# Inverse transform's second stage in two-step pieces, residual sum and stores moved behind it, and a new set of due times

## The chip, the cores and the metric

The kernel runs on one core of one Trainium2 chip. The metric is the device time of one execution in microseconds (us), compared as medians over runs. The core's engines are named as in the profile: PE is the matrix engine (PEld its weight loads), DVE the vector engine, ACT the scalar engine with its function tables, SP the queue that issues all DMA transfers here. POOL does nothing of weight.

## The reference, cut to what matters

The input is one sequence `x` of 2048 positions by 512 channels. Its layer norm feeds two branches: a state-space convolution, whose kernel of 2048 taps per channel is summed from 128 complex exponentials and applied by FFT, and a token-and-channel mixer with two small MLPs. Their product is added to the input.

```python
xn = _layernorm(x, axis=-1)
s = _A_ref(xn, ...)     # K = einsum(C, exp(dt A l), dt B).real; y = irfft(rfft(K) * rfft(u)); y + u * Dskip
g = _silu(_B_ref(xn, B_w1, B_w2, B_w3, B_w4))   # spatial-shift mixing, then the channel MLP
return x + s * g
```

## The kernel before

Position is split as (t, r, s): s has 16 values and is called a step here, r has 4, t has 32. A tile over 128 partitions holds r and t; `X` (line 459) holds all 16 steps by 512 channels in SBUF and is rewritten in place: input, then its layer norm, then the mixer's residual stream, then its Silu, then the result.

The program is not issued in the order in which it is written. Every call on an engine is recorded in a `Plan` with an estimated cost, the tiles it touches and a due time (`due(t)`, line 536). `Plan.order` (line 220) then runs a list scheduler: on the engine that comes free first it picks, among the operations whose inputs its model holds ready, the one with the smallest due time, and adds penalties: `SWITCH` for an ACT operation that needs another function table, `PREFER` or `AVOID` for an operation that either ACT or DVE may do (class `Either`). `LAND` and `PAD` are the model's latencies of a DMA and of a signal between engines. The order that comes out is fixed; at run time each engine works through its own list and waits on signals. So a changed due time or buffer moves rows on all four engines.

The stages, in words:

- Loads, layer norm, `h_pair`, `u_stage1`, `hs_pair`: token mixing, and the first stage of the input's transform (written to DRAM as `scr_Ud`).
- `tables(hf)` for two halves of the channels (256 each), eight chunks of 32 channels per half: ACT and DVE make tables of exponentials, sines and cosines (tiles `mag`, `pt`, `kt`, `eg`), PE multiplies them into the convolution kernel (`pc<-kt`, `pc<-pt`), which goes to DRAM (`scr_Kda`, `scr_Kdb`).
- `kstage1(hf)`: first transform stage of that kernel, through DRAM (`ksl` in, `scr_Kfa`/`scr_Kfb` out).
- `products(hf)`: second stage of both transforms, complex product, first inverse stage; its results go to DRAM (`scr_Zda`, `scr_Zdb`). The second half has eight units.
- `mlp(g)`, g = 0..7: the channel MLP on two steps of `X` each (`pb<-x1T,w3h`, `ghl`, `pa<-w4h,ghl`, then `X<-pa`). It fills PE between the stages above.
- `gate(g)`: Silu of two steps. `finish(hf, q)`: second inverse stage, product with the gate, residual sum, store.

`finish` works on four steps of one half of the channels. It loads 2 x 512 KB of `scr_Zda` or `scr_Zdb` into `zin` (a ring of two buffers of 1 MB, `zinr`), and four slices of the input into `xr` (a ring of two, `xrr`); PE fills a pair of PSUM banks; DVE multiplies both into `X`, adds `xr`, and four stores of 128 KB follow, in runs of 1 KB. The pairs alternate between the banks `pc` and `pd` (`pp_pair`, line 524). A read of a DRAM scratch tensor waits for all writes to that tensor, so no `scr_Zdb` load starts before the last unit of `products(1)` has stored.

Of the kernel before, what the change touches and what calls it, by code (L numbers as in the profile page):

```python
# [10 lines left out]
F32 = mybir.dt.float32  # L11
# [8 lines left out]
P = 128  # L20
L = 2048
D = 512
# [72 lines left out]
SAME = {"PE": 0.0, "ACT": 0.13, "DVE": 0.1, "SP": 0.0}  # L95
TABLE_LOAD = 1.41
DMA_RATE = 300e3
LAND, PAD = 4.17, 0.21
BASE, FINE, END = 16512, 19840, 229368

KGC = 3.25
SWITCH = 70.05
PREFER, AVOID = 182.71, 8.67
PV, T0, TC = 91.3, -48.6, 81.82
M0, MC, WC = 233.6, 235.8, 0.05
H0, HC, SC = -706.8, 114.13, 0.09
KA, PA, PAC, FA = 159.4, -391.4, 0.1, 834.5
KB, PB, PBC, FB = 90.8, 491.3, 0.06, 203.3
FC = 0.06


def mlp_due(g, jp):
# [3 lines left out]
class Plan:  # L116
# [103 lines left out]
    def order(self):  # L220
# [17 lines left out]
        while len(out) < len(ops):  # L238
# [4 lines left out]
            for o in pools[e]:  # L243
                if o.ready <= t + 0.02:
                    v = o.vt
                    if e == "ACT" and o.table and o.table != table:
                        v += SWITCH
                    if len(o.alts) > 1:
# [140 lines left out]
def kernel(  # L389
# [8 lines left out]
    plan = Plan(nc)  # L398
    V, A, T, Q = [Engine(plan, e) for e in ("DVE", "ACT", "PE", "SP")]
    E = Either(plan)  # L400

    xv = u[0].rearrange("(t r s) d -> r t s d", r=4, s=S)
    ov = out[0].rearrange("(t r s) d -> r t s d", r=4, s=S)
# [5 lines left out]
    DH = D // 2  # L409
    Kd = [dram.tile([P, NCH, L2, 4], F32, name=f"scr_Kd{h}") for h in "ab"]  # L410
    K1d = [dram.tile([4, 2 * NG, L2, DH // 4], F32, name=f"scr_Kf{h}") for h in "ab"]
    Zd = [dram.tile([4, S, 2, NG, DH], F32, name=f"scr_Zd{h}") for h in "ab"]
# [4 lines left out]
    def area(nbytes):  # L417
        o = place[0]
        place[0] = o + nbytes
        assert place[0] <= END  # L420
        return o

    def at(offset, shape, dt, name):
        return nc.alloc_sbuf_tensor_at(name, shape, dt, offset=offset)[:]

    def keep(shape, name, dt=F32):
        n = 4
        for k in shape[1:]:
            n *= k
        return at(area((n + 31) // 32 * 32), shape, dt, name)  # L430
# [20 lines left out]
    is2 = keep([P, L1], "is2")  # L451
# [7 lines left out]
    X = at(area(4 * S * D), [P, S, D], F32, "X")  # L459
    K2, K4 = 2048, 4096  # L460
# [8 lines left out]
    early = area(11 * K2)  # L469
# [7 lines left out]
    late = place[0]  # L477
# [17 lines left out]
    o = late + 8 * K4  # L495
# [9 lines left out]
            pr=Ring(o, K4, 4), kh=Ring(o + 4 * K4, K4, 2), z1e=Ring(o + 6 * K4, K4, 3),  # L505
        ),
    ]
    zinr = Ring(early, 2 * K4, 2)
    xrr = Ring(o + 10 * K4, K4, 2)
    assert o + 12 * K4 <= END  # L510


# [11 lines left out]
    def pp_pair():  # L524
        turn["pp"] += 1
        return bank[2 + turn["pp"] % 2]
# [9 lines left out]
    def due(t):  # L536
        plan.vt = t


    def by_r(sb, dr, to_dram=False):  # L540

        for r in range(4):
            a, d = sb[32 * r : 32 * r + 32], dr[r]
            Q.dma_start(d, a) if to_dram else Q.dma_start(a, d)
# [311 lines left out]
    def gate(g):  # L856
        due(FA + FC * g)
        X2 = X[:, 2 * g : 2 * g + 2]
        A.activation(X2, X2, AF.Silu)

    def finish(hf, q):
        due((FA, FB)[hf] + FC * q)
        s0 = 4 * q
        ch = slice(hf * DH, hf * DH + DH)
        zin = zinr([P, 2, 4, DH], F32, "zin")
        for k in range(2):
            s = s0 + 2 * k
            Q.dma_start(zin[:, k], Zd[hf][:, s : s + 2, :, :, :].rearrange("r s e g d -> (s e g) r d"))
        xr = xrr([P, 4, DH], F32, "xr")
        by_r(xr, xv[:, :, s0 : s0 + 4, ch])  # L870
        X4 = X[:, s0 : s0 + 4, ch]
        py = [t.rearrange("p (b d) -> p b d", b=2) for t in pp_pair()]
        with plan.together(cost=1.1):
            for k in range(2):
                for r in range(4):
                    for a in range(2):
                        h = slice(64 * a, 64 * a + 64)
                        T.matmul(py[a][32 * r : 32 * r + 32, k], is2[h], zin[h, k, r], start=True, stop=True)
        for a in range(2):
            V.tensor_mul(X4[:, a::2], X4[:, a::2], py[a])  # L880
        V.tensor_add(X4, X4, xr)
        by_r(X4, ov[:, :, s0 : s0 + 4, ch], to_dram=True)


    def pow2_scale(cols, dst_s, dst_inv, target):
# [273 lines left out]
    for g in range(8):  # L1159
        gate(g)  # L1160
    for hf in range(2):
        for q in range(4):
            finish(hf, q)
    with nc.allow_non_contiguous_dma(reason="parameters by state"), tc.manual_schedule():
        make_identity(nc, ident)
        plan.issue(tc)
# [24 lines left out]
```

## Time and profile before

| | us |
|---|---|
| median of 3 runs | 700.04 |
| the runs | 699.28, 700.04, 702.01 |
| the profiled execution | 700.67 |
| span of the profiled execution, first to last instruction | 698.9 |
| PE busy in the span | 626.0 |
| DVE busy | 546.3 |
| ACT busy | 461.8 |

Rows of the profile name an operation by the tiles it writes and reads (`X<-X,xr`), with the count of merged instructions behind an x. In a row of the timeline the first number is the start from the beginning of the span, the second the time covered; what stands in brackets is the engine's idle time just before, and what ended it. All recorded operations are issued from one line, so all rows carry L279 and are told apart by tile. A float32 matmul appears as two instructions. "SPq" rows are DMA issues; the time to landing of a transfer is given apart. Matmul ends are modelled.

### The profile page before, as it was taken

The numbers are of one execution on the slowest core, as the hardware profiler recorded it, in microseconds if no ns is written. First come the engines' busy times: TensorE is split into PE (matmuls) and PEld (weight loads), VectorE is DVE, ScalarE is ACT, GpSimd is POOL, SyncE is SP. The second block draws the span as 40 slices with busy tenths as digits, with TensorE's granted clock in tenths as the row PEclk, the third lists the DMA queues.
The fourth block names the chain that finished last, engine by engine and source line by source line (L and its number), as shares of the span: only waits on it lengthen the run. The fifth ranks groups of instructions, "written<-read, shape, count | busy, mean of one in ns | idle before, by whom it ended". The sixth has DMA issues, their size and how long they took to land.

```text
span 698.9 us, 13611 instructions
## 1 busy us (share of the span) xinstructions
PE 626.0 (90%) x5446; PEld 411.3 (59%) x5446; DVE 546.3 (78%) x766; ACT 461.8 (66%) x1021; POOL 0.7 (0%) x6
## 2 busy tenths in 40 slices
PE   0898998899997988898999999899999999999951
PEld 0477677548446657556757676667556666666610
DVE  4969969889999999999989999986433464566452
ACT  3987899988757999998979898763245341213410
POOL 0000000000000000000000000000000000000000
PEclk9999999899999999999999999999999999999975
DMA  9953334311202110365334343355869457631997
GB/s 248 246 202 102 131 118 132 107 69 54 68 31 64 59 50 28 68 173 158 109 106 121 100 123 106 99 143 153 205 175 339 112 142 179 184 121 48 304 290 204
DMA packets 107663, 95.60 MB, mean 137 GB/s; under 512 B 48912, under 2 KB 89872, under 8 KB 107216
## 3 DMA queue, kind: packets, MB, share of 16 engines
q1 hardware_dynamic: 107600, 94.73, 47.5%
q8 instruction: 43, 0.70, 0.4%
q14 instruction: 20, 0.16, 0.1%
HBM read 61.16 MB, written 33.55 MB: 136 GB/s over the span
## 4 chain that ended last, share of the span: by engine, by line
PE 52%; DVE 28%; ACT 10%; DMA 5%; issue 3%; SPq 1%; ACTq 0%; DVEq 0%
PE pb L279 19%; PE pa L279 14%; PE pd L279 11%; DVE pt L279 9%; PE pc L279 8%; DVE kt L279 4%; ACT L279 2%; DVE X L279 2%; DVE stats L279 2%; ACT mag L279 2%; DVE eg L279 2%; DVE w4h L279 1%; SPq L279 1%; ACT pt L279 1%; DVE pab L279 1%
## 5 line engine op out<-in xcount | busy, mean ns | idle before, releaser
L279 PE MATMUL pa<-w4h,ghl 128*128 128x512 f16 (+1 forms) x528 | 124.0, 383 | 4.8 <-DVE ghl L279 2.7
L279 PE MATMUL pb<-x1T,w3h 128*128 128x256 f16 (+1 forms) x1056 | 124.2, 274 | 3.2 <-ACT g L279 2.3
L279 PEld LDWEIGHTS <-w3h 128*128 128x128 f16 (+1 forms) x1056 | 102.8, 100 | 28.6 <-issue 13.4
L279 ACT ACT_TABLE_LOAD x75 | 96.2, 1283 | 6.3 <-DMA wst<-in_B_w_dram 5.0
L279 PEld LDWEIGHTS <-ghl 128*128 128x128 f16 (+1 forms) x528 | 49.4, 98 | 72.0 <-issue 15.3
L279 ACT ACTIVATE mag<-par 128x64 f32<-128x64 f32 x512 | 86.3, 281 | 6.5 <-DVE pt L279 3.5
L279 PE MATMUL pc<-kt 128*32 128x64 f32 x1024 | 84.0, 417 | 4.1 <-DVE kt L279 2.5
L279 PE MATMUL pc<-pt 128*32 128x64 f32 x1024 | 77.9, 388 | 2.6 <-DVE pt L279 2.6
L279 ACT ACTIVATE g<-pb,wsc 128x512 f32<-128x512 f32 (+1 forms) x48 | 31.4, 666 | 66.0 <-PE pb L279 64.5
L279 PE MATMUL pb<-xT,w 128*128 128x256 f32 x256 | 61.7, 401 | 0.8 <-ACT xT L279 0.7
L279 DVE SCALAR_TENSOR_TENSOR ghl<-g,wsc,ghl 128x512 f16<-128x512 f32 (+1 forms) x48 | 34.8, 727 | 30.6 <-ACT ghl L279 30.3
L279 PEld LDWEIGHTS pb<-xT,w 128*128 128x128 f32 x256 | 50.5, 201 | 13.6 <-ACT xT L279 2.6
L279 PEld LDWEIGHTS pc<-kt 128*32 128x32 f32 x1024 | 48.4, 178 | 16.4 <-issue 12.2
L279 PEld LDWEIGHTS pc<-pt 128*32 128x32 f32 x1024 | 56.2, 195 | 3.0 <-DVE pt L279 2.9
L279 DVE TENSOR_TENSOR kt<-mag,kt 128x1024 f32<-128x1024 f32 x32 | 41.3, 1292 | 0.0
L279 DVE TENSOR_TENSOR pr<-pd,kh 128x512 f32<-128x512 f32 x48 | 33.4, 726 | 8.4 <-PE pd L279 8.0
L279 DVE SCALAR_TENSOR_TENSOR pt<-kt,pt 128x2080 f32<-128x2080 f32 x16 | 38.1, 2389 | 0.2
L279 ACT ACTIVATE kt<-kt,halfpi 128x2080 f32<-128x2080 f32 x16 | 35.6, 2224 | 0.0
L279 ACT ACTIVATE pt<-pt 128x2080 f32<-128x2080 f32 x16 | 34.2, 2139 | 2.0 <-DVE kt L279 1.8
L279 PE MATMUL pb<-w,hT 128*128 128x512 f32 x58 | 29.2, 649 | 3.1 <-ACT hT L279 3.1
L279 ACT ACTIVATE ghl<-g,wsc 128x512 f16<-128x512 f32 (+1 forms) x42 | 28.9, 697 | 4.4 <-PE pa L279 2.1
L279 ACT ACTIVATE kt<-pt 128x2080 f32<-128x2080 f32 x12 | 24.1, 2007 | 10.7 <-DVE pt L279 10.7
(157 smaller groups left out, 906.9 us busy)
## 6 DMA issues: line engine op xcount, KB each, us to landing
wst<-in_B_w_dram SPq DMA_DIRECT2D x20, 512.0 KB, 3.9
scr_Ud<-ue SPq DMA_DIRECT2D x16, 512.0 KB, 4.4
scr_Kfa<-k1e SPq DMA_DIRECT2D x16, 256.0 KB, 3.3
uin<-scr_Ud SPq DMA_DIRECT2D x32, 128.0 KB, 2.9
cst<-c_gp SPq DMA_DIRECT2D x16, 256.0 KB, 2.8
kin<-scr_Kfa SPq DMA_DIRECT2D x32, 128.0 KB, 2.5
scr_Zda<-z1e SPq DMA_DIRECT2D x16, 256.0 KB, 3.4
xr<-in_A_u_dram SPq DMA_DIRECT2D x32, 128.0 KB, 4.0
```

The lines of the kernel that those rows point to most:

```text
L279: ins = [getattr(self.engines[op.eng], name)(*args, **kw).ins for name, args, kw in op.calls]
```

## The change

`finish(hf, q)` is split. `inverse(hf, g)` works on two steps of one half of the channels: one load of 512 KB into a `zin` of its own (a ring of five for the first half, of eight for the second), 16 instead of 32 matmul rows, and two DVE products of 256 columns. `finish(g)` then adds the residual for two steps over all 512 channels and stores them in four transfers of 128 KB, now in runs of 4 KB. The input for the residual is loaded per four steps over all channels, 16 transfers of 256 KB instead of 32 of 128 KB, into four buffers that are not reused.

All due times, the three penalties and the model's `LAND` and `PAD` are replaced by another set.

```diff
-LAND, PAD = 4.17, 0.21
+LAND, PAD = 3.32, 0.17
...
-SWITCH = 70.05
-PREFER, AVOID = 182.71, 8.67
...
+SWITCH = 135.33
+PREFER, AVOID = 290.89, 121.33
...
-    zinr = Ring(early, 2 * K4, 2)
-    xrr = Ring(o + 10 * K4, K4, 2)
+
+    zinr = [Ring(early, K4, 5), Ring(o, K4, 8)]
+    xrs = [late + 2 * K4 * k for k in range(3)] + [o + 10 * K4]
...
-    def finish(hf, q):
-        due((FA, FB)[hf] + FC * q)
-        s0 = 4 * q
+    def inverse(hf, g):
+        due((FA, FB)[hf] + FC * g)
         ch = slice(hf * DH, hf * DH + DH)
-        zin = zinr([P, 2, 4, DH], F32, "zin")
-        for k in range(2):
-            s = s0 + 2 * k
-            Q.dma_start(zin[:, k], Zd[hf][:, s : s + 2, :, :, :].rearrange("r s e g d -> (s e g) r d"))
-        xr = xrr([P, 4, DH], F32, "xr")
-        by_r(xr, xv[:, :, s0 : s0 + 4, ch])
...
+        zin = zinr[hf]([P, 4, DH], F32, "zin")
+        Q.dma_start(zin, Zd[hf][:, 2 * g : 2 * g + 2, :, :, :].rearrange("r s e g d -> (s e g) r d"))
+        py = [t[:, :DH] for t in pp_pair()]
+        with plan.together(cost=0.55):
+            for r in range(4):
+                for a in range(2):
+                    h = slice(64 * a, 64 * a + 64)
+                    T.matmul(py[a][32 * r : 32 * r + 32], is2[h], zin[h, r], start=True, stop=True)
         for a in range(2):
-            V.tensor_mul(X4[:, a::2], X4[:, a::2], py[a])
-        V.tensor_add(X4, X4, xr)
-        by_r(X4, ov[:, :, s0 : s0 + 4, ch], to_dram=True)
+            Xh = X[:, 2 * g + a, ch]
+            V.tensor_mul(Xh, Xh, py[a])
+
+    xr = []
+
+    def finish(g):
+        due(FB + FC * g)
+        if g % 2 == 0:
+            xr.append(at(xrs.pop(), [P, 4, D], F32, "xr"))
+            by_r(xr[-1], xv[:, :, 2 * g : 2 * g + 4])
+        X2 = X[:, 2 * g : 2 * g + 2]
+        V.tensor_add(X2, X2, xr[-1][:, 2 * (g % 2) : 2 * (g % 2) + 2])
+        by_r(X2, ov[:, :, 2 * g : 2 * g + 2], to_dram=True)
...
     for hf in range(2):
-        for q in range(4):
-            finish(hf, q)
+        for g in range(8):
+            inverse(hf, g)
+    for g in range(8):
+        finish(g)
```

What the new numbers do to the program is seen in its order. Three places matter here.

The first is the SP queue at the end of the program, which issues every transfer in this order. `zin`, `xr` are loads, `scr_Zdb<-z1e` the second half's stores from `products(1)`, `out_dram<-X` the result. Before:

```order
L279 DMA zin<-scr_Zdb 128x4x256 x2
L279 DMA xr<-in_A_u_dram 32x4x256 x4
L279 DMA out_dram<-X 32x4x256 x4
L279 DMA zin<-scr_Zdb 128x4x256 x4
L279 DMA out_dram<-X 32x4x256 x4
L279 DMA xr<-in_A_u_dram 32x4x256 x8
L279 DMA zin<-scr_Zdb 128x4x256 x2
L279 DMA out_dram<-X 32x4x256 x12
L279 DMA xr<-in_A_u_dram 32x4x256 x4
L279 DMA out_dram<-X 32x4x256 x4
```

And now:

```order
L279 DMA scr_Zdb<-z1e 128x1024
L279 DMA xr<-in_A_u_dram 32x2048 x2
L279 DMA scr_Zdb<-z1e 128x1024
L279 DMA xr<-in_A_u_dram 32x2048 x6
L279 DMA zin<-scr_Zda 128x4x256
L279 DMA xr<-in_A_u_dram 32x2048 x2
L279 DMA scr_Zdb<-z1e 128x1024
L279 DMA xr<-in_A_u_dram 32x2048 x2
L279 DMA zin<-scr_Zda 128x4x256 x2
L279 DMA zin<-scr_Zdb 128x4x256 x8
L279 DMA out_dram<-X 32x1024 x32
```

Loads and stores alternated before; now all eight loads of the second half stand in one row behind the last `scr_Zdb` store, and all 32 stores behind them. The `xr` loads stand ahead of both (the first four of the sixteen far earlier).

The second is DVE's list from the last accumulation of the MLP on (`X<-pa`). Rows with `pc` or `pd` are products of the inverse stage, rows with `xr` residual sums. Before:

```order
L279 SCALAR_TENSOR_TENSOR X_87<-pa1_91,wsc_76,X_87 128x512
L279 TENSOR_TENSOR X_87<-X_87,pd0_96 128x2x256
L279 TENSOR_TENSOR X_87<-X_87,pd1_97 128x2x256
L279 TENSOR_TENSOR X_87<-X_87,xr_617 128x4x256
L279 TENSOR_TENSOR X_87<-X_87,pc0_94 128x2x256
L279 TENSOR_TENSOR X_87<-X_87,pc1_95 128x2x256
L279 TENSOR_TENSOR X_87<-X_87,xr_615 128x4x256
```

And now:

```order
L279 TENSOR_TENSOR X_87<-X_87,xr_624 128x1024
L279 SCALAR_TENSOR_TENSOR X_87<-pa0_90,wsc_76,X_87 128x512
L279 TENSOR_TENSOR X_87<-X_87,pd0_96 128x256
L279 TENSOR_TENSOR X_87<-X_87,pd1_97 128x256
L279 SCALAR_TENSOR_TENSOR X_87<-pa1_91,wsc_76,X_87 128x512
L279 TENSOR_TENSOR X_87<-X_87,xr_625 128x1024
L279 TENSOR_TENSOR X_87<-X_87,pd0_96 128x256
L279 TENSOR_TENSOR X_87<-X_87,pd1_97 128x256
L279 TENSOR_TENSOR X_87<-X_87,xr_626 128x1024
```

One residual sum now stands ahead of the last accumulation. Behind `X<-pa0` stand eight pairs of products of 256 columns and seven residual sums in turn, where behind `X<-pa1` there had been five pairs of 512 columns and five sums.

The third is SP again, at the round trip through DRAM between the last tables and `products(1)`: `scr_Kdb<-kev` is the last piece of the convolution kernel, `ksl` its load, `scr_Kfb<-k1e` the transformed kernel, `kin` its load. Before:

```order
L279 DMA scr_Kdb<-kev 128x256
L279 DMA scr_Zda<-z1e 128x512
L279 DMA ksl<-scr_Kdb 128x16x128 x2
L279 DMA scr_Zda<-z1e 128x512
L279 DMA scr_Kfb<-k1e 64x2x1024 x2
L279 DMA zin<-scr_Zda 128x4x256 x4
L279 DMA scr_Kfb<-k1e 64x2x1024 x6
L279 DMA uin<-scr_Ud 64x4x256 x2
L279 DMA kin<-scr_Kfb 128x4x64 x20
```

And now:

```order
L279 DMA scr_Kdb<-kev 128x256
L279 DMA scr_Zda<-z1e 128x512
L279 DMA ksl<-scr_Kdb 128x16x128 x2
L279 DMA zin<-scr_Zda 128x4x256 x5
L279 DMA scr_Kfb<-k1e 64x2x1024 x8
L279 DMA uin<-scr_Ud 64x4x256 x2
L279 DMA kin<-scr_Kfb 128x4x64 x20
```

Five loads of the first half's inverse stage now stand ahead of all eight `scr_Kfb` stores, where four had stood behind two of them.

More of the change, by code (lines that the diff above doesn't have):

```diff
@@ L97 @@
 DMA_RATE = 300e3
-LAND, PAD = 4.17, 0.21
+LAND, PAD = 3.32, 0.17
 BASE, FINE, END = 16512, 19840, 229368
 KGC = 3.25
-SWITCH = 70.05
-PREFER, AVOID = 182.71, 8.67
[L104 to L109, printed above, removed]
+SWITCH = 135.33
+PREFER, AVOID = 290.89, 121.33
+PV, T0, TC = 366.3, -80.6, 92.61
+M0, MC, WC = 302.7, 225.43, 0.24
+H0, HC, SC = -1212.9, 183.55, 0.09
+KA, PA, PAC, FA = -108.1, -1278.7, 0.07, 1091.5
+KB, PB, PBC, FB = -40.0, -299.0, 0.06, 186.2
+FC = 0.16
 def mlp_due(g, jp):
@@ L859, in gate @@
         A.activation(X2, X2, AF.Silu)
-    def finish(hf, q):
-        due((FA, FB)[hf] + FC * q)
-        s0 = 4 * q
+    def inverse(hf, g):
+        due((FA, FB)[hf] + FC * g)
         ch = slice(hf * DH, hf * DH + DH)
-        zin = zinr([P, 2, 4, DH], F32, "zin")
-        for k in range(2):
-            s = s0 + 2 * k
-            Q.dma_start(zin[:, k], Zd[hf][:, s : s + 2, :, :, :].rearrange("r s e g d -> (s e g) r d"))
-        xr = xrr([P, 4, DH], F32, "xr")
-        by_r(xr, xv[:, :, s0 : s0 + 4, ch])
[L871 to L878, printed above, removed]
-        for a in range(2):
-            V.tensor_mul(X4[:, a::2], X4[:, a::2], py[a])
-        V.tensor_add(X4, X4, xr)
-        by_r(X4, ov[:, :, s0 : s0 + 4, ch], to_dram=True)
+        zin = zinr[hf]([P, 4, DH], F32, "zin")
[6 more added lines that the diff above has]
+                    T.matmul(py[a][32 * r : 32 * r + 32], is2[h], zin[h, r], start=True, stop=True)
+        for a in range(2):
+            Xh = X[:, 2 * g + a, ch]
[9 more added lines that the diff above has]
+        by_r(X2, ov[:, :, 2 * g : 2 * g + 2], to_dram=True)
     def pow2_scale(cols, dst_s, dst_inv, target):
```

## The prediction

> **What bounds the kernel now.** I read the page first, then the busy times by stretches, then the timeline of the end, and last the groups and transfers that price the edits.
>
> ```profile
> span 698.9 us, 13611 instructions
> PE 626.0 (90%) x5446; PEld 411.3 (59%) x5446; DVE 546.3 (78%) x766; ACT 461.8 (66%) x1021; POOL 0.7 (0%) x6
> ```
>
> PE is busy 626.0 of 698.9 us, so 73 us are left to win at most as long as PE's work stays, and the change leaves every matmul in place. Where these 73 us lie, the stretches say; after the bounds come the length and then, for each engine, its busy time.
>
> ```profile
> core 0: us, PE busy (x) PEld busy (x) DVE busy (x) ACT busy (x) POOL busy (x), PEclk, DMA share, GB/s
> 150.00:290.00 140.00, 128.47 (x1177) 85.55 (x1175) 139.93 (x161) 115.89 (x299) 0.00 (x0) 0.98 0.20 56
> 290.00:475.00 185.00, 177.39 (x1808) 119.11 (x1809) 176.61 (x214) 157.07 (x346) 0.00 (x0) 0.97 0.43 120
> 475.00:645.80 170.80, 170.46 (x1366) 107.66 (x1364) 86.31 (x138) 55.45 (x83) 0.00 (x0) 1.00 0.59 165
> 645.80:667.60 21.80, 21.80 (x232) 13.67 (x238) 9.05 (x12) 8.73 (x12) 0.00 (x0) 1.00 0.99 297
> 667.60:698.90 31.30, 7.46 (x128) 1.88 (x127) 13.23 (x17) 1.06 (x1) 0.00 (x0) 0.59 0.86 244
> ```
>
> From 475 to 667.6 PE is full, and DVE and ACT are half idle: PE alone sets the pace. From 150 to 475 PE and DVE are both nearly full (DVE 139.9 of 140, then 176.6 of 185), and PE has 11.5 and 7.6 us idle. In the last 31.3 us PE works 7.5 and DVE 13.2 us: no engine is the bound there. That end is the place to read row by row.
>
> ```profile
> 643.84 2.00 PE L279 MATMUL pc<-pr,cst 64*128 64x256 f32 x16
> 647.00 0.38 SPq L279 DMA_DIRECT2D scr_Zdb<-z1e  x1
> 663.51 4.06 PE L279 MATMUL pa<-w4h,ghl 128*128 128x512 f16 x18
> 666.96 1.41 DVE L279 SCALAR_TENSOR_TENSOR X<-pa,wsc,X 128x512 f32<-128x512 f32 x2 [2.82 <-PE pa L279]
> 673.19 5.32 SPq L279 DMA_DIRECT2D xr<-in_A_u_dram  x8
> 674.71 1.29 DVE L279 TENSOR_TENSOR X<-X,pc 128x512 f32<-128x512 f32 x2 [1.03 <-PE pc L279]
> 678.60 0.93 SPq L279 DMA_DIRECT2D zin<-scr_Zdb  x2
> 679.88 8.73 SPq L279 DMA_DIRECT2D out_dram<-X  x12
> 681.77 2.50 DVE L279 TENSOR_TENSOR X<-X,xr 128x1024 f32<-128x1024 f32 x2 [2.96 <-DMA xr<-in_A_u_dram]
> 684.27 1.11 PE L279 MATMUL pc<-zin,is 64*32 64x256 f32 x16 [6.84 <-DVE X L279]
> 688.65 1.95 SPq L279 DMA_DIRECT2D xr<-in_A_u_dram  x4
> 693.01 1.23 DVE L279 TENSOR_TENSOR X<-X,xr 128x1024 f32<-128x1024 f32 x1 [4.98 <-DMA xr<-in_A_u_dram]
> 694.26 1.78 SPq L279 DMA_DIRECT2D out_dram<-X  x4
> ```
>
> The last product of the second half ends on PE at 645.84 and its store goes out at 647.00. The MLP's last matmuls end at about 667.57, the accumulation starts at 666.96. From there it is one chain: `xr` loads queue on SP behind stores (673.19), DVE waits for them until 681.77, only then the last `zin` load has been fetched into a buffer that was in use, PE gets it at 684.27, twelve stores hold SP until 688.6, the last `xr` load goes out behind them, DVE gets it at 693.01, and the last stores leave from 694.26. From the accumulation to the end of the span: 698.9 - 666.96 = 31.9 us, of which DVE works some 14.
>
> **The change: the end.** The new order cuts that chain in two places. The residual input is loaded ahead of the last `scr_Zdb` store into buffers of its own, so no `xr` load stands behind a store, and all eight `zin` loads of the second half have a buffer, so none waits for a product. What is left behind `X<-pa` is DVE's own list: two accumulations, eight pairs of products of 256 columns, seven residual sums.
>
> ```profile
> L279 DVE TENSOR_TENSOR X<-X,xr 128x1024 f32<-128x1024 f32 x8 | 9.8, 1225 | 8.2 <-DMA xr<-in_A_u_dram 7.9
> L279 DVE COPY kev<-pc 128x256 f32<-128x256 f32 x6 | 2.5, 409 | 0.0
> L279 DVE COPY k1e<-pc 128x512 f32<-128x512 f32 x4 | 2.8, 690 | 4.8 <-PE pc L279 4.8
> ```
>
> The two accumulations took 1.41 us together (row 666.96), a residual sum of 1024 columns 1.225. A product of 256 columns out of PSUM isn't in the trace; the nearest row is the PSUM copy of the same size, 0.409. The bounds are half of a pair of 512 (1.29 us in row 674.71, so 0.32 each) and that copy of 512, 0.69. I take 0.41, the row of equal size. DVE's list is then 1.41 + 16 x 0.41 + 7 x 1.225 = 16.5 us (15.1 to 21.0 by the bounds). From the last residual sum to the end of the span it now takes 698.9 - 694.24 = 4.7 us for the last four stores, which stays. I add 1 us for one wait between banks like the one in front of row 674.71. The end behind the accumulation: 16.5 + 4.7 + 1 = 22.2 us instead of 31.9, so **-9.7**.
>
> [...]
>
> Two covers have to hold for this. First, the MLP must still end when it does. PE's rows from the last product to the last `pa` matmul:
>
> ```profile
> 649.52 4.10 PE L279 MATMUL pb<-x1T,w3h 128*128 128x256 f16 x36
> 667.50 1.09 PE L279 MATMUL pd<-zin,is 64*32 64x256 f32 x32
> ```
>
> There were 84 `w3h`, 42 `w4h` and 48 inverse instructions counted as the program lists them; now 72, 42 and 64. A `w3h` row costs 4.10 / 36 = 0.114, a `w4h` row 4.06 / 18 = 0.226 (row 663.51), an inverse row, two instructions, 1.09 / 16 = 0.068: 22.3 against 22.0 us. Nothing changes, if the one piece of the second half ahead of the last MLP matmuls has its data. Second, the transfers must arrive.
>
> ```profile
> scr_Zdb<-z1e SPq DMA_DIRECT2D x8, 512.0 KB, 4.3
> zin<-scr_Zdb SPq DMA_DIRECT2D x8, 512.0 KB, 6.7
> out_dram<-X SPq DMA_DIRECT2D x32, 128.0 KB, 3.4
> ```
>
> Store landing 4.3 us, load landing 6.7: the first `zin` piece needs 1.2 + 4.3 + 6.7 = 12.2 us from the end of the last product, and PE asks for it after 72 x 0.114 + 30 x 0.226 + 56 x 0.068 = 18.8. Behind that product there remain about 1 MB of `xr`, 0.5 of `scr_Zdb`, 1.5 of first-half `zin`, 4 of second-half `zin` and 4 of stores, 11 MB; at the 297 GB/s of the stretch 645.8 to 667.6 that is 37 us, where DVE's end comes 21.1 + 16.5 + 4.7 + 1 = 43.3 us after that product. So the transfers are just hidden; if they run at the 244 GB/s of the last stretch, they take 45 and set the end. The 32 stores need SP 0.45 us each when the queue is free (row 694.26: 1.78 for four), 1.8 per residual sum, against 2.05 us of DVE work; at the 0.73 us of row 679.88 they take 2.9 and are the bound.
>
> **The change: the stretch before.** The due times move rows everywhere, but the stages keep their places on PE. Between equal operations of ACT and DVE the choice falls differently: DVE gets two more `kt<-pt` rows and four more `kev` copies, and loses three `w3h` rows; nine other small rows more and eleven fewer, of 0.4 to 0.8 us, I take as even.
>
> ```profile
> L279 DVE TENSOR_SCALAR kt<-pt 128x2080 f32<-128x2080 f32 (+1 forms) x14 | 18.7, 1338 | 0.1
> L279 DVE TENSOR_SCALAR w3h<-wst,wsc 128x1024 f16<-128x1024 f32 (+1 forms) x4 | 2.6, 649 | 0.0
> 342.51 1.23 DVE L279 TENSOR_TENSOR kt<-mag,kt 128x1024 f32<-128x1024 f32 x1
> 344.74 0.67 PE L279 MATMUL pc<-kt 128*32 128x64 f32 x8
> ```
>
> 2 x 1.338 + 4 x 0.409 - 3 x 0.649 = **+2.4 us** on DVE. In the stretch where DVE is full this has no cover: chunk 11's last table row ends at 343.74, and its matmuls start at 344.74, so PE has 1.0 us of slack and later only waits that it can't make up from 475 on. Below, the bound is a gain: the last two blocks of `kt`/`pt` matmuls now stand behind about 12 us more of other PE work, which could fill the 7.6 us of PE's idle time from 290 to 475. Above, DVE's list up to chunk 10's last table row is longer by three `kt<-pt`, three `k1e` copies and the four `kev` copies less the same three `w3h`: 4.0 + 2.1 + 1.6 - 1.9 = 5.8 us. I take +2.4, the sum over the whole list, since by the last chunk the difference is back there; -7.6 and +5.8 go into the range.
>
> **The change: the round trip through DRAM.** Behind the last `kt`/`pt` matmuls the kernel goes out and in twice.
>
> ```profile
> 489.29 0.63 PE L279 MATMUL pc<-pt 128*32 128x64 f32 x8
> 515.37 0.22 DVE L279 TENSOR_TENSOR ksl<-ksl,Dt 128x64 f32<-128x64 f32 x1
> 517.01 1.09 PE L279 MATMUL pc<-ksl,ks 32*64 32x512 f32 x8
> 527.76 1.04 PE L279 MATMUL pd<-ksl,ks 32*64 32x512 f32 x8
> 555.16 1.95 PE L279 MATMUL pd<-kin,cst 128*64 128x256 f32 x16
> 542.46 2.56 SPq L279 DMA_DIRECT2D kin<-scr_Kfb  x5
> kin<-scr_Kfb SPq DMA_DIRECT2D x32, 128.0 KB, 2.9
> ```
>
> It is 515.37 - 489.92 = 25.5 us until DVE may touch `ksl`, and PE had 27.1 us of other work until 517.01. Now PE has 108 `w3h`, 30 `w4h` and some 5 us of product rows there: 12.3 + 6.8 + 5 = 24.1, so 1.4 us of wait at most. Then from the end of that stage (528.8) to the first `kin` matmul 26.4 us of cover, with the load issued at 542.46. Now the cover is 72 x 0.114 + 48 x 0.226 + 3 = 22 us; the data took 542.46 + 2.0 for four of the five loads + 2.9 to land - 528.8 = 18.6. I take nothing for both, since five `zin` loads instead of four pass while the stage computes and no longer stand between the `scr_Kfb` stores; at worst 1.4 + 5 us.
>
> **Sum.** 698.9 - 9.7 + 2.4 = 691.6 us of span; 1.8 us lie around it (700.67 - 698.9), so 693.4 for the profiled execution. The median of the runs is 0.6 below that execution: **692.8**, taken as 692.5.
>
> **Rivals.**
> - *The stretch before gains as well.* For it: PE's 7.6 us idle from 290 to 475, and more PE work ahead of the last tables. Against it: DVE is full there and gets work. 692.5 - 2.4 - 5 = 685.
> - *The stores are the new bound.* SP issues all 32 in a row behind eight loads; at 0.73 us each they last 23.4 us from the first residual sum (at about 667 on the old clock), plus 4.7 - 1.78 = 2.9 to land: 693.3 instead of 689.2 for the end, so 696.5. For it: row 679.88 and DMA shares of 0.86 to 0.99; against it: those stores were runs of 1 KB and some had to wait for DVE.
> - *The second half starves, slower.* Place: PE in front of chunk 10 and 11's matmuls and at the round trip. Price: 5.8 - 1.0 for the late tables, 1.4 for `ksl`, and `kin` late by one more store landing each for the five `zin` loads that share the queue, up to 10 us. From 13 us on it eats the gain of 9.7 and the noise: 692.5 - 2.4 + 16 = 706. It decides if the cover of 22 us in front of `kin` is too short by more than 8 us; by the rows it is long enough by 3.
> - *The change does not do what it says*: the early second-half piece on PE waits for its load and holds the MLP's last twelve rows back. By the rows it has 6 us to spare; if the 2.5 MB ahead of it cost 8.4 us at 297 GB/s, it is 2.5 us late: 695.
>
> **How the numbers follow.** Forecast (688.5 to 696) 0.54; gain before the end as well, 685: 0.16; stores as the bound, 696.5: 0.12; piece late, 695: 0.07; starved, 706: 0.11. A measurement of this kernel tells about 0.5%, 3.5 us, from no change: faster is below 696.5, slower above 703.5. Faster: 0.54 + 0.16 + 0.07 and a third of the stores' 0.12 make 0.80, taken as 0.78; slower 0.10; the same 0.12. The range that leaves out no more than two in ten runs from 683 to 701; the forecast's own is 688.5 to 696.
>
> **What would show it.** Right: DVE's rows behind the last `X<-pa` follow each other with gaps under 0.3 us and no wait for `xr`; the end behind the accumulation is 21 to 24 us; PE is full from 475 on up to the MLP's end. Wrong: residual sums that wait for PE behind `zin` (transfers bound), stores of 0.7 us on SP with DVE long done (stores bound), idle time of PE in front of `ksl` or `kin` rows, or an MLP end that isn't within 3 us of 670 (the stretch before decides).

## The result: 679.3 us, faster by 3%, and the profile after

| | before | after |
|---|---|---|
| median of 4 runs each, same chip | 700.92 us (699.28 to 702.01) | 679.25 us (678.81 to 680.51) |
| ratio | | 0.970, 95% interval 0.967 to 0.972 |
| profiled execution, span | 700.67, 698.9 us | 679.28, 677.5 us |
| first accumulation `X<-pa` of the last MLP | 666.96 | 656.20 |
| from there to the end of the span | 31.9 | 21.3 |

692.5 us was forecast. The end came as worked out (22.2 us forecast, 21.3 measured). The whole miss lies ahead of the accumulation: +2.4 us was forecast there, and it came 10.8 us earlier. First the page of the changed kernel, its busy times:

```profile
span 677.5 us, 13618 instructions
PE 624.4 (92%) x5446; PEld 408.0 (60%) x5446; DVE 547.8 (81%) x783; ACT 459.2 (68%) x1020; POOL 0.7 (0%) x6
```

No engine's work changes by much: DVE has 1.5 us more than before, PE 1.6 and ACT 2.6 less. So the 21 us are idle time that went away. The stretches say where it went. The changed kernel, columns as in the prediction's table (bounds, length, PE, PEld, DVE, ACT, POOL, clock, DMA):

```profile
25.00:150.00 125.00, 119.90 (x826) 84.58 (x828) 116.16 (x207) 116.28 (x264) 0.00 (x0) 0.99 0.43 139
150.00:290.00 140.00, 126.99 (x1138) 83.80 (x1130) 139.87 (x164) 117.59 (x294) 0.00 (x0) 0.99 0.18 53
290.00:475.00 185.00, 182.37 (x1886) 123.10 (x1887) 173.85 (x211) 153.89 (x351) 0.00 (x0) 0.99 0.46 126
475.00:640.00 165.00, 165.00 (x1339) 102.78 (x1331) 81.46 (x134) 54.15 (x80) 0.00 (x0) 1.00 0.68 185
640.00:656.20 16.20, 16.20 (x150) 8.71 (x148) 5.70 (x13) 5.08 (x7) 0.00 (x0) 1.00 1.07 317
656.20:677.50 21.30, 8.91 (x115) 2.50 (x113) 15.47 (x26) 1.06 (x1) 0.00 (x0) 0.63 0.86 257
```

And the one stretch of the kernel before that the prediction did not show:

```profile
25.00:150.00 125.00, 115.48 (x734) 80.97 (x733) 105.68 (x195) 112.02 (x257) 0.00 (x0) 0.95 0.42 135
```

From 25 to 150 us DVE did 10.5 us more than before, PE 4.4 more, ACT 4.3 more. From 290 to 475 PE did 5.0 more. From 475 to the accumulation PE is full in both.

The granted clock of PE rose too, from 0.960 to 0.981 over the span. That doesn't account for the 10.8 us: PE's busy time ahead of the accumulation was 617.9 us before and 615.4 after, and 615.3 in a second profile of the kernel before.

The end, DVE and SP of the changed kernel:

```profile
656.20 0.75 DVE L279 SCALAR_TENSOR_TENSOR X<-pa,wsc,X 128x512 f32<-128x512 f32 x1
657.49 0.75 DVE L279 TENSOR_TENSOR X<-X,pd 128x256 f32<-128x256 f32 x2 [0.54 <-PE pd L279]
...
671.19 1.22 DVE L279 TENSOR_TENSOR X<-X,xr 128x1024 f32<-128x1024 f32 x1
656.24 18.34 SPq L279 DMA_DIRECT2D out_dram<-X  x32
```

One wait of 0.54 us is left (gaps under 0.3 were forecast), none for `xr`. A pair of products of 256 columns takes 0.75 us, and the list ends at 671.19 + 1.22 = 672.41, 16.2 us behind the start of the accumulation. SP issues the 32 stores in 18.34 us, but a single store holds it for only 0.42 us (the median), and for 6.2 us it waits for DVE's sums. The span ends 5.1 us behind DVE's list. PE's rows for the two covers of the prediction:

```profile
632.53 2.00 PE L279 MATMUL pc<-pr,cst 64*128 64x256 f32 x16
653.45 0.66 PE L279 MATMUL pd<-zin,is 64*32 64x256 f32 x16
```

The first second-half piece runs 19 us after the last product, without a wait.

### The profile page after: what moved, and what is told of

The parts are those of the page before. It is cut to its first block, busy times and chain, and to the rows that moved or that the text cites. A ratio compares the mean times of both kernels' runs of the same rounds, so it can differ in the third digit from the quotient of the medians.

```text
span 677.5 us, 13618 instructions
## 1 busy us (share of the span) xinstructions
PE 624.4 (92%) x5446; PEld 408.0 (60%) x5446; DVE 547.8 (81%) x783; ACT 459.2 (68%) x1020; POOL 0.7 (0%) x6
## 4 chain that ended last, share of the span: by engine, by line
PE 46%; DVE 39%; ACT 6%; issue 5%; DMA 2%; SPq 1%; ACTq 0%
PE pb L279 16%; PE pa L279 13%; DVE pt L279 11%; PE pd L279 9%; DVE kt L279 8%; PE pc L279 7%; DVE X L279 4%; DVE pab L279 2%; DVE eg L279 2%; DVE stats L279 2%; ACT mag L279 2%; ACT L279 2%; DMA X<-in_A_u_dram 1%; DVE w4h L279 1%; DVE pr L279 1%
## 5 line engine op out<-in xcount | busy, mean ns | idle before, releaser
L279 ACT ACTIVATE mag<-par 128x64 f32<-128x64 f32 x512 | 83.8, 270 | 5.5 <-DVE kt L279 4.2
L279 PE MATMUL pb<-xT,w 128*128 128x256 f32 x256 | 59.8, 394 | 1.5 <-DVE xT L279 1.0
L279 ACT ACTIVATE kt<-kt,halfpi 128x2080 f32<-128x2080 f32 x16 | 33.1, 2067 | 0.0
L279 ACT ACTIVATE pt<-pt 128x2080 f32<-128x2080 f32 x16 | 31.6, 1973 | 0.1
L279 ACT ACTIVATE ghl<-g,wsc 128x512 f16<-128x512 f32 (+1 forms) x43 | 30.6, 724 | 1.6 <-ACT g L279 0.9
L279 DVE BATCH_NORM_STATS2 stats<-X 128x6 f32<-128x512 f32 x32 | 22.0, 705 | 8.0 <-DMA X<-in_A_u_dram 7.5
L279 PE MATMUL pa<-w,hT 128*128 128x512 f32 x58 | 26.5, 597 | 0.0
```

Source lines behind the costliest of these rows:

```text
L279: ins = [getattr(self.engines[op.eng], name)(*args, **kw).ins for name, args, kw in op.calls]
```

## The experiments

Times are ratios to the kernel before, run beside each kernel on the same chip. "Mixing ends" is the start of the last matmul instruction of token mixing (`pa` or `pb<-w,hT`), "end" the time from the first accumulation to the end of the span; both come from the profiled runs.

| kernel | mixing ends | accumulation | end | ratio, 95% interval |
|---|---|---|---|---|
| before | 208.0 | 666.96 | 31.9 | 1 |
| before, profiled again | 206.8 | 665.41 | 34.2 | one execution |
| new structure, old numbers | 205.8 | 665.88 | 19.1 | 0.983 (0.978 to 0.987) |
| old structure, new numbers | 200.3 | 657.22 | 29.4 | 0.986 (0.981 to 0.990) |
| new numbers early, old late | 198.5 | 661.67 | 19.7 | 0.978 (0.973 to 0.982) |
| old numbers early, new late | 208.0 | 664.49 | 21.2 | 0.982 (0.977 to 0.987) |
| after | 199.9 | 656.20 | 21.3 | 0.970 (0.967 to 0.972) |
| after, again | 199.8 | 657.03 | 21.5 | 0.971 (0.967 to 0.975) |

### Structure or numbers

Edit of the first: the changed kernel with the old constants (`LAND, PAD`, `SWITCH` to `FC`); of the second: the kernel before with the new ones.

```diff
-LAND, PAD = 3.32, 0.17
+LAND, PAD = 4.17, 0.21
-SWITCH = 135.33
+SWITCH = 70.05
...
```

> The new structure (pieces of two steps, sums and stores at the end) with the old numbers of the planner (due times, penalties, landing estimate). The times named are of the profiled runs: before 700.7 us, with the accumulation of the MLP at 666.96 and 31.9 us behind it; after 679.3, 656.2 and 21.3. Order theory (the 10.8 us ahead of the accumulation come from the planner's numbers alone): accumulation at 666 to 668, 21 to 22 us behind it, time 690. Structure theory (the new pieces free PE or the queues earlier on): accumulation at 656 to 658, time 680.

> The old structure with the new numbers of the planner. Order theory: accumulation at 655 to 658, 31 to 33 us behind it, time 690, and together with the run above the two gains add up to 21 to 22 us. Structure theory: accumulation at 666, time 700.

> The changed kernel itself, beside the others on the same chip. The four combinations of structure and numbers so far: new structure with old numbers 0.983 of the time before, old structure with new numbers 0.986, new structure with new numbers early and old ones late 0.978, the reverse 0.982. If the gains add up, both together are 0.969 (0.983 x 0.986); the first comparison gave 0.970.

The order theory holds. With the old numbers the accumulation stays at 665.88 and the end falls to 19.1 us (one residual sum more runs ahead of the accumulation there); with the new numbers and the old structure the accumulation is at 657.22 and the end stays at 29.4. The ratios multiply: 0.983 x 0.986 = 0.969. So the restructured end is worth 1.7%, and the due times, which the prediction had as a small loss, 1.4%.

### Early or late

The planner keeps both sets of numbers and changes from one to the other when the last matmul of token mixing is placed.

```diff
-                    v = o.vt
+                    v = o.vt[now]
...
+            left -= pick.early
+            if now == 0 and left == 0:
+                now = 1
+                globals().update(SETS[1])
```

> The new structure; the planner uses the new numbers until the last matmul of token mixing is placed, from there on the old ones. Early theory (some 8 of the 10.8 us are won ahead of the end of token mixing, where ACT's order kept PE and DVE waiting, and everything behind shifts by that): last token mixing matmul at 200 us instead of 208, accumulation at 659 to 660, time 682 to 683. Late theory (the shift at 208 us is eaten by the stretch in which DVE is full, and the gain is made by the later order, with more of PE's work ahead of the last tables): last token mixing matmul at 200, but accumulation at 665 to 667, time 689.

> The mirror image: old numbers until the last matmul of token mixing is placed, then the new ones, with the new structure. Early theory: last token mixing matmul at 208, accumulation at 663 to 664, time 686 to 687. Late theory: last token mixing matmul at 208, accumulation at 656 to 658, time 680.

Both runs are nearer to the early theory: 0.978 and 0.982, 683.95 and 687.07 us. Split at the end of mixing, the table reads simply. New early numbers bring that end from 206 to 208 down to 198.5 to 200.3, in every kernel that has them. From there to the accumulation it takes 456 to 457 us with the new late numbers and 459 to 460 with the old ones, 463 where the old late numbers follow the new early ones, a state they were not chosen for. So of the 10.8 us some 8 lie ahead of 208 us and 2 to 3 behind.

### What the early numbers won

DVE's waits from 25 to 150 us (engine, tile, releaser: us in total, times, longest), in the kernel before:

```profile
DVE rawA L279 <- ACT mag L279: 4.2, 1, 4.2
DVE X L279 <- PE pb L279: 3.8, 1, 3.8
DVE pt L279 <- ACT pt L279: 3.7, 2, 3.1
```

and in the changed one:

```profile
DVE ue L279 <- PE pa L279: 3.7, 3, 3.2
DVE xT L279 <- PE pd L279: 2.0, 1, 2.0
DVE pt L279 <- ACT pt L279: 1.7, 1, 1.7
```

Two of the three waits of before are for ACT directly, and the 3.8 us for PE have ACT behind them: the prediction's stretch table starts at 150, where DVE is full, and so did not show any of this. The theory is that behind 150 us DVE's list sets the pace, so what counts is how much of it is done by then. The profiles fit it: where DVE did 105.7 to 108.7 us of work from 25 to 150 us (the kernel before twice, and three kernels with the old early numbers), mixing ended at 205.8 to 208.0; where it did 116.2 to 117.0 (four with the new ones), at 198.5 to 200.3.

First the most visible of these waits was taken away: in the kernel before, 32 exponentials on ACT held back the last two Gelu instructions, and with them PE's first mixing matmuls. The edit takes these two `mag` groups (`held`) out of the finished order and puts them back behind the last Gelu, ahead of the next sine (k).

```diff
+        out = [o for o in out if o not in self.held]
...
+        out[k:k] = self.held
```

> The kernel before with one move on ACT alone: the last 32 mag exponentials of the second block (128.4 to 133.2 us) are placed behind the last two Gelu instructions of token mixing and the two copies behind them, which costs one table load more (1.28 us). Nothing moves on the other engines. Idle theory (DVE sets the pace from 142 us on; what was won early is its idle time, 3.8 us of which stand behind these Gelu): PE starts the first token mixing matmuls at 132 instead of 135.2 us and runs the first eight in 3.7 instead of 6.5 us, DVE's gap at 141.7 us closes, the last of them ends 3 to 5 us earlier than 208.0, time 3 to 5 us less, ratio 0.993 to 0.996. Rival (what counts is where the tables stand, not this wait): the sines that now start some 6 us later starve DVE instead, the last token mixing matmul stays within 1 us of 208, ratio 0.999 to 1.004.

PE's rows in that kernel, against the kernel before, where these eight matmuls started at 135.18 and took 6.51 us:

```profile
131.54 3.70 PE L287 MATMUL pb<-w,hT 128*128 128x512 f32 x8
...
144.61 0.58 PE L287 MATMUL pd<-m,ones 1*128 1x1 f32 x2 [3.98 <-ACT m L287]
145.12 9.50 PE L287 MATMUL pa<-w,hT 128*128 128x512 f32 x16
```

The first part came as expected, at full clock and 3.6 us earlier, and won nothing. ACT's list, now one table load longer, is late with the next thing: PE waits 3.98 us for `m` and DVE 3.2 us for the sines. Behind that wait PE's clock is at 0.50, so that 16 mixing matmuls take 9.50 us instead of 7.13, and mixing ends at 207.9. ACT is 99% busy from 85 to 130 us in the kernel before, so moving one instruction in its list moves the wait.

The time, 0.996 (0.994 to 0.999), is 2.7 us less all the same. In the profiles that gain lies behind 208 us (accumulation at 661.74), and neither theory has it. Some 1.6 us of it go with the clock: behind a wait of 1.96 us the kernel before ran at 0.51 from 441.2 to 444.7 us; this one, behind a wait of 1.97 us at the same place, stayed at 1.00. From there to the accumulation it took 224.3 us, against 225.9 in both profiles of the kernel before. The cause of the rest stays open.

> The kernel before, profiled a second time, for how far one profiled execution can be trusted: the profile of the kernel before had the last token mixing matmul at 208.0 and the accumulation at 666.96, and a kernel that differs from it by one move on ACT had 207.9 and 661.7. If the stretch from 208 us on varies by itself, the accumulation comes at 661 to 666 with the last token mixing matmul again at 208; if it doesn't, at 666 to 668.

The second profile of the kernel before says how far one execution can be trusted: mixing 1.2 us and accumulation 1.6 us earlier than in the first. Differences under 2 us between single profiles are no evidence by themselves.

Then the theory itself was tested with DVE work that does nothing, ahead of 150 us in front of DVE's gaps, and behind 150 us where it has none: the finished order's calls are repeated, in the first kernel those of two `ue` copies and two absolute values, in the second those of three `eg` products.

```diff
+        for o in ue[3:5] + [ab[0], ab[2]]:
+            o.calls = o.calls * 3
```

> The kernel before with DVE work repeated three times in front of three gaps of DVE ahead of 150 us: two ue copies at 42.7, the absolute values at 87.8 and 136.7 us, 2 x 2 x 0.62 and 2 x 2 x 1.14 = 7.0 us more in all, before gaps of 4.2, 3.1 and 3.8 us. Nothing else changes. Idle theory (DVE has room ahead of 150 us): the gaps swallow it, last token mixing matmul at 208 to 209.5, time within 2 us, ratio 0.998 to 1.003. Rival (these gaps lie on the path too, so DVE's work counts everywhere): last token mixing matmul 6 us or more later, ratio 1.008 to 1.010.

> The same amount of work, placed where DVE has no gap: three eg products (152.5, 174.6 and 203.7 us) repeated three times, 6 x 1.13 = 6.8 us. Idle theory (behind 150 us DVE's list sets the pace, and what comes late there stays late up to the end): last token mixing matmul 5 to 7 us later than 208, time 5 to 7 us more, ratio 1.007 to 1.010. Rival (PE's or ACT's list sets the pace, DVE is only busy in their shadow): less than 2 us, ratio 0.998 to 1.003.

The early work gave 0.999 (0.997 to 1.002), the late work 1.011 (1.008 to 1.013): 7 us for 6.8 us of work. The gaps take the early work as a whole; DVE in that kernel:

```profile
42.10 4.18 DVE L285 COPY ue<-pa 128x512 f32<-128x512 f32 x6
47.48 0.69 DVE L285 TENSOR_TENSOR rawA<-rawA,tm 128x512 f32<-128x512 f32 x1 [1.11 <-ACT mag L285]
```

Four copies more, and the wait of 4.2 us has shrunk to 1.1. One point of the late run missed: mixing ended only 2.1 us later than in the second profile (208.9), not 5 to 7; the rest shows at the accumulation (671.21 against 665.41). So DVE's list is the pace from 150 us on (tested with work at 152 to 204 us), and its idle time ahead of that, 19.3 us before and 8.8 after, is where the early 8 us came from. Which of the planner's numbers did it was not separated.

### The end: which cut does what

```diff
-    zinr = [Ring(early, K4, 5), Ring(o, K4, 8)]
+    zinr = [Ring(early, K4, 5), Ring(o, K4, 2)]
```

> The changed kernel with two buffers instead of eight for the zin pieces of the second half; the order up to the MLP's end is the same, behind it a load follows the matmuls that free its buffer. Chain theory (loads that wait for a buffer were the first cut in the chain): five pieces come late in three rounds of about 8 us (6.7 us of landing, the matmuls, the queue), the last one at about 680 us, and the end behind the accumulation is 28 to 32 us instead of 21.3: time 6 to 10 us above the changed kernel, ratio to before 0.978 to 0.985. Rival (the stores or the bytes set the end anyway): 21 to 23 us, ratio 0.97.

```diff
-    xrs = [late + 2 * K4 * k for k in range(3)] + [o + 10 * K4]
+    xrs = [o + 10 * K4] * 4
```

> The changed kernel with one place instead of four for the residual input xr; three of its four loads now stand behind stores and wait for sums. Chain theory (xr loads behind stores were the second cut): three rounds of 8 stores on SP (4.6 us), 4 to 5 us of landing and two sums (2.5 us), the end behind the accumulation 36 to 42 us instead of 21.3, time 14 to 20 us above the changed kernel, ratio to before 0.990 to 0.998. Rival (the products and the bytes set the end): within 3 us of the changed kernel, ratio 0.970 to 0.974.

With two `zin` buffers the end is 30.3 us (28 to 32 expected), ratio 0.983 (0.980 to 0.986): this cut alone is worth 8 us. With one place for `xr` it is 49.6 us (36 to 42 expected), 1.011 (1.008 to 1.014), slower than before. DVE there, a round every 12.4 us:

```profile
672.66 2.36 DVE L279 TENSOR_TENSOR X<-X,xr 128x1024 f32<-128x1024 f32 x2 [5.03 <-DMA xr<-in_A_u_dram]
685.08 2.36 DVE L279 TENSOR_TENSOR X<-X,xr 128x1024 f32<-128x1024 f32 x2 [10.06 <-DMA xr<-in_A_u_dram]
697.38 2.36 DVE L279 TENSOR_TENSOR X<-X,xr 128x1024 f32<-128x1024 f32 x2 [9.94 <-DMA xr<-in_A_u_dram]
```

The round was sized about right (11 to 12 us). The estimate of the end left out what lies around the three rounds: 6.2 us from the accumulation to the first of them, and 7.8 us from the start of the last two sums to the end of the span. Sums and stores at the end pay only together with the early loads.

Last, is DVE's list really the bound of the 21.3 us? Two sums went to POOL.

```diff
-        V.tensor_add(X2, X2, xr[-1][:, 2 * (g % 2) : 2 * (g % 2) + 2])
+        (G if g in (3, 5) else V).tensor_add(X2, X2, xr[-1][:, 2 * (g % 2) : 2 * (g % 2) + 2])
```

> The changed kernel with two of the eight residual sums (steps 6, 7 and 10, 11) on POOL, which is idle; DVE's list behind the accumulation is 2 x 1.13 = 2.3 us shorter, nothing else moves. If DVE's list sets the end, as the sum in the prediction has it, and a sum on POOL takes up to 3 us: the end behind the accumulation 19 us instead of 21.3, time 2 us less than the changed kernel, ratio to before 0.967. If the 32 stores on SP (18.3 us in a row at 0.57 each) or the landing of data set it: no change, ratio 0.970; if POOL is slower than that, the stores queue behind it on SP and the time rises.

The ratio is 0.973 (0.970 to 0.977): no gain. The end even grew to 23.4 us; SP now waits 1.4 us for POOL. In that kernel, DVE and POOL:

```profile
667.12 0.75 DVE L279 TENSOR_TENSOR X<-X,pc 128x256 f32<-128x256 f32 x2 [1.23 <-PE pc L279]
669.11 0.75 DVE L279 TENSOR_TENSOR X<-X,pc 128x256 f32<-128x256 f32 x2 [1.23 <-PE pc L279]
669.90 1.87 DVE L279 TENSOR_TENSOR X<-X,xr 128x1024 f32<-128x1024 f32 x1
666.03 4.66 POOL L279 TENSOR_TENSOR X<-X,xr 128x1024 f32<-128x1024 f32 x2 [664.73 <-DMA out_dram<-X]
```

The last four pieces all use the one pair of banks `pc`, so PE waits for DVE's product and DVE for PE's next: 0.75 + 1.23 = 1.98 us a piece. In the changed kernel a sum of 1.23 us fills exactly that wait. Two bounds of the same length lie on top of each other, and removing one shows the other.

The hand-over was that long at half of PE's clock. In the changed kernel the 16 matmuls of a piece took 0.66 us at 653.45, at a granted clock of 1.00, and 1.44 at 668.90, at 0.50:

```profile
668.90 1.44 PE L279 MATMUL pc<-zin,is 64*32 64x256 f32 x16 [0.56 <-DVE X L279]
670.41 0.75 DVE L279 TENSOR_TENSOR X<-X,pc 128x256 f32<-128x256 f32 x2
```

DVE's product starts 1.51 us behind the first matmul here, and 0.75 us behind it at 653.45. With the full clock a piece would take some 1.2 us (an estimate: 1.98 - 1.51 + 0.75), and DVE's list alone would be the bound; no run tested that.

### One operation, two prices

While the stretches were compared, DVE's rows showed two durations for one form. DVE in the kernel before, and PE beside it:

```profile
155.90 1.22 DVE L279 TENSOR_TENSOR pt<-pt,eg 128x1024 f32<-128x1024 f32 x1
157.03 1.67 DVE L279 TENSOR_TENSOR kt<-mag,kt 128x1024 f32<-128x1024 f32 x1
157.18 0.69 PE L279 MATMUL pc<-kt 128*32 128x64 f32 x8
```

The jump comes as PE starts the table matmuls. Their operands are one channel's column through a table laid out by rows: elements 128 bytes apart. The next kernel gives them neighbouring elements instead of `w[:, top, q]` and `w[:, :L2, q]`, and changes nothing else. It leaves out the right operands, so it doesn't compute the convolution kernel; its time is a price and not a usable result.

```diff
+            calls = plan.ops[-1].alts["PE"][1]
+            for k, (name, (dst, _, _), kw) in enumerate(calls):
+                q, w = 16 * dh + 4 * (k // 8) + k % 4, (kt, pt)[k // 4 % 2]
+                calls[k] = name, (dst, w[:, L2 + 1 + q], w[:, 2 * q : 2 * q + 2].rearrange("p a q -> p (a q)")), kw
```

> The changed kernel with other operands in the 32 groups of table matmuls (pc<-kt, pc<-pt): instead of one channel's column through all rows of the table (elements 128 bytes apart) each reads as many elements that lie side by side, the same number of matmuls of the same shapes in the same order on every engine. The tables' product, and with it the output, is wrong. In the changed kernel 20 DVE products of 1024 columns that ran while PE did these matmuls took 1.73 us on average, the 96 others 1.22; in the kernel before six sines on ACT took 2.84 there, the 41 others 1.98. If the reading of scattered elements by PE is what slows DVE and ACT: products 1.2 to 1.3 there, DVE, which is full from 130 to 475 us, gets through its list up to 28 us sooner (some 93 us of such matmuls from 146 us on, times 0.3), of which PE can use at most the 21 us that it idles from 25 to 475: time 8 to 18 us less than the changed kernel, ratio to before 0.945 to 0.96. If it is anything else about these stretches: 1.7 us as before, ratio 0.970.

The ratio is 0.931 (0.925 to 0.937), 650.7 us. That is more than expected. The estimate had left out that PE's own table matmuls became twice as fast (with `pc<-pt`, 162 us of busy time became 68); how the gain divides between that and the faster neighbours was not separated. Groups of the changed kernel (busy us, mean ns):

```profile
L279 PE MATMUL pc<-kt 128*32 128x64 f32 x1024 | 84.2, 416 | 2.7 <-DVE kev L279 1.4 <-DVE kt L279 0.6 <-ACT kev L279 0.6
L279 DVE TENSOR_TENSOR kt<-mag,kt 128x1024 f32<-128x1024 f32 x32 | 42.4, 1324 | 0.0
```

and of this one:

```profile
L279 PE MATMUL pc<-kt 128*32 128x64 f32 x1024 | 34.3, 233 | 9.1 <-DVE X L279 5.8 <-DVE kev L279 3.2 <-issue 0.2
L279 DVE TENSOR_TENSOR kt<-mag,kt 128x1024 f32<-128x1024 f32 x32 | 38.8, 1213 | 0.0
```

DVE's products beside the matmuls fell to 1.22 us (from 1.73 in the mean), and ACT's longest row of 2080 columns to 2.03 us (from 2.48). So the scattered reading by PE had cost three engines time. Next a layout that keeps the result: `pt`, `kt` and `eg` by channel, in every instruction that touches them; `mag`, `EB` and `pab` stay by row.

```diff
+    def laid(t):
+        return t.rearrange("p r q -> p (r q)").rearrange("p (q r) -> p q r", q=CQ)
...
+                calls[i] = name, (dst, w[:, q, top], w[:, q, :L2]), kw
```

The second kernel has besides:

```diff
-KGC = 3.25
+KGC = 1.75
```

> The changed kernel, with the tables kt, pt and eg laid out by channel (the rows of one channel side by side) instead of by row. It computes the same as the changed kernel, and every engine keeps its order. PE now reads elements side by side, as in e12_contiguous, where PE's table matmuls took 0.219 us instead of 0.416 and DVE's products beside them 1.22 instead of 1.73; the magnitudes mag, EB and pab keep their layout, so four products, one eg and one sum per chunk read one operand on DVE with elements 256 bytes apart. If DVE reads those at the same pace: 650 to 654 us, ratio 0.930 to 0.936. If scattered reading slows DVE as it does PE (0.5 us for each of 96 instructions, 48 us in the stretch where DVE is full): 675 to 695 us, ratio 0.965 to 0.995.

> The same layout, with the planner told that a group of table matmuls costs 1.75 us instead of 3.25, so that the order on every engine is made anew. In e12_contiguous PE waited some 46 us from 25 to 475 us, most of it for DVE, with an order made for matmuls of twice the length. If the order is the limit now: 3 to 10 us less than e13_rows_inside. If DVE's list is: within 2 us of it.

The ratios are 1.025 (1.022 to 1.029) and 1.013 (1.009 to 1.018): both are slower than the kernel before. In the first of the two:

```profile
L279 DVE TENSOR_TENSOR kt<-mag,kt 128x1024 f32<-128x1024 f32 x32 | 62.1, 1940 | 0.0
L279 DVE TENSOR_TENSOR eg<-EB 128x1024 f32<-128x1024 f32 x16 | 32.3, 2019 | 0.0
```

DVE's scattered reads took longer too, by 0.73 to 0.80 us per 1024 elements (1.94 and 2.02 us, against 1.21 and 1.22 in the kernel with neighbouring operands). A new order wins 9 us of that back and no more. So all tables by channel (`EB`, `pab` and `kab` like `mag`), which leaves scattered writes to ACT alone, and in a second kernel new numbers for the planner:

```diff
-        pt = phtile([P, L2 + 1 + L1, CQ], "pt")
+        pt = phtile([P, CQ, L2 + 1 + L1], "pt")
...
-        mag = at(magn, [P, L2, BQ], F32, "mag")
+        mag = at(magn, [P, BQ, L2], F32, "mag")
...
-KGC = 3.25
+KGC = 1.75
```

```diff
-SWITCH = 135.33
-PREFER, AVOID = 290.89, 121.33
+SWITCH = 144.57
+PREFER, AVOID = 303.32, 103.47
...
```

> The changed kernel with every table by channel: kt, pt and eg as in e13_rows_inside, and EB, pab and mag as well, so that PE and DVE read side by side everywhere; what is scattered now is what ACT writes, 64 elements 256 bytes apart in each of 512 mag exponentials and 48 bytes apart in 96 EB exponentials. The first block's exponentials have to wait until the raw parameters, which lie at the same place, are dead. The order is the planner's own, with 1.75 us for a group of table matmuls. It computes the same as the changed kernel. If ACT writes scattered elements at its old pace (0.24 to 0.27 us per mag exponential): DVE's products back at 1.22, 645 to 665 us, ratio 0.92 to 0.95. If ACT pays as PE and DVE do (0.1 us more for each, 51 us more on ACT): 665 to 690 us.

> The same kernel with the planner's numbers chosen for this layout (due times and penalties alone differ). If the order is the limit there: 5 to 10 us less than e15_all_by_channel. If DVE's list is: within 3 us of it.

The ratio is 0.928 (0.924 to 0.932), 649.8 us; with numbers chosen for it 0.916 (0.912 to 0.921), 641.7 us. The second beats both kernels: 59 us under the kernel before beside it, some 38 under the changed one. ACT's exponentials in the first of them, and in the kernel with neighbouring operands:

```profile
L279 ACT ACTIVATE mag<-par 128x64 f32<-128x64 f32 x512 | 80.2, 303 | 0.8 <-DVE pt L279 0.6
```

```profile
L279 ACT ACTIVATE mag<-par 128x64 f32<-128x64 f32 x512 | 77.1, 244 | 4.3 <-DVE kt L279 3.7 <-DVE pt L279 0.5
```

ACT took 0.06 us more for a scattered write of 64 elements in the mean (0.303 against 0.244), but only 3.1 us more of busy time in all: these instructions overlapped (512 of 0.303 us cover 80.2 us). The order was the limit too: 8.1 us between the last two kernels.

## Why the prediction was right and wrong

- **The change: the end**, -9.7 forecast, -10.6 measured. DVE's list took 16.2 us with its one wait of 0.54 in it (16.5 and 1 forecast), the last stores 5.1 (4.7). A product of 256 columns lasts 0.416 us in the mean, as the copy did (0.409); but two in a row overlap and cover 0.75, so that the sum was a little too long. The smaller products have a small price: a pair of 256 columns covered 0.75 us, where half of a pair of 512 had covered 0.65 (1.29 for the pair). What the step did not see is that the hand-over between PE and DVE on one bank pair, with PE's granted clock at 0.50, is as long as the list (1.98 us a piece).
- **The covers** held. The first second-half piece ran 19 us after the last product (18.8 forecast) without a wait; PE was full from 475 us to the accumulation, so **the round trip through DRAM** cost nothing, as said; the transfers stayed hidden, at 317 and 257 GB/s; a store held SP for 0.42 us in the median, near the 0.45 of the working, and SP waited 6.2 us for DVE.
- **The change: the stretch before** is the step that failed: +2.4 forecast, -10.8 measured (-8.4 between the second profiles of both kernels). I compared two lists of DVE rows, found one longer by 2.4 us, and argued that DVE is full from 150 to 475 us, so that there is no cover. That DVE is full there is true, and the late added work shows that it has no cover (7 us for 6.8). But where an engine's list is the pace, the time is its work plus its idle time ahead of that stretch, and I never opened 25 to 150 us. DVE idled 19.3 us there, and 8.8 after. Counting rows could only give the small term.
- The lower bound of that step, -7.6, had the right sign, but it named the smaller part. PE's idle time from 290 to 475 did fall, from 7.6 to 2.6 us; the runs that split early from late put what lies behind 208 us at 2 to 3 us of the 10.8.
- Of the rivals, "the stretch before gains as well" (685) had the direction, at half the size and by its late part only. "The stores are the new bound", "the second half starves" and "the change does not do what it says" are refuted by the rows above.
- **What would show it** worked as a pointer: an MLP end more than 3 us off 670 was to mean that the stretch before decides, and its last accumulation started at 658.16.

## What to carry to other kernels

Before a list of rows is compared on an engine that is full, look at its idle time ahead of the full stretch, and at what releases it there: a new order is worth first what it moves into that room. Where two dependent loops lie on top of each other, test by removing one of them before the sum is believed. And compare the durations of one form of instruction over the whole trace: here two prices of one product, 1.22 and 1.67 us, led to the matmuls beside it, and the first layout tried against them made DVE's products slower (1.94 us), so check a layout for every engine that touches the data.

## What the runs showed of the hardware

- **Scattered reads slowed the reader and its neighbours.** Fp32 matmuls of 64 columns took 0.388 and 0.416 us in the mean with elements 128 bytes apart (`pc<-pt`, `pc<-kt`) and 0.231 and 0.233 side by side. In the kernel before, DVE products of 1024 columns that lay in such matmuls took 1.61 to 1.94 us (16 rows), those clear of them 1.34 at most and 1.22 in the mean (some 100 rows); ACT rows of 2080 columns, most of them sines, took 2.84 (6 rows) against 1.98 (some 40 rows). With neighbouring operands both effects went: the longest of these products took 1.23 us, the longest ACT row 2.03. DVE as the scattered reader, with elements 256 bytes apart, took 1.94 to 2.02 us against 1.21. What causes it, no run here shows.
- **The clock after a wait.** In the kernel before eight mixing matmuls took 6.51 us behind a wait of 3.07 us, at a granted clock of 0.55, in its second profile 5.40 behind 3.35; in the kernel with the new structure and old numbers, which has the same lists up to there, 3.70 behind 2.89. The length of the wait alone didn't decide in these runs: behind 1.96 us the kernel before ran at 0.51 from 441 us on, and the kernel with the exponentials moved stayed at 1.00 behind 1.97. Where the clock was kept in those eight matmuls, mixing ended at 205.8 us, else at 206.8 and 208.0; so the clock may have been worth up to 2 of the 8 us (an estimate from these three ends).
- **A sum on POOL** of 1024 columns took 2.33 us, where DVE took 1.23, and DVE's own sum beside it 1.87.
